# Joined transposing transfers, two kinds of square buffers and new transfer clocks in a gated-attention and token-mixer kernel

## The chip, the core and the metric

The kernel runs on one core of a Trainium2 chip. The core has a matmul engine (PE, with its weight loads shown apart as PEld), three elementwise engines (DVE, ACT and POOL), and SP, whose queue here issues most of the transfers that 16 DMA engines carry out. The metric is the time on the device of one execution, in microseconds, as the median of several runs.

## What is computed

Eight batches of 3200 rows pass through two stages. `u` and `v` have 256 columns, `z` has 64.

```python
scores = (1.0 / S) * np.matmul(z, z.transpose(0, 2, 1))
attn = np.maximum(scores, 0.0) ** 2
x = u * np.matmul(attn, v)
wq, wk = x @ w_q, x @ w_k
W_tok = (1.0 / np.sqrt(64)) * np.einsum('bsd,btd->bst', wq, wk)
mixed = np.einsum('bst,btd->bsd', W_tok, x)
out = np.maximum(mixed, 0.0) @ w_out
```

The score matrix is symmetric, since both factors are `z`. The second stage has no nonlinearity between its two products, so it is computed as wq times the small matrix that wk and x make together (the "heads"), without the matrix of 3200 x 3200.

## The kernel before

**Tiles.** A batch has 25 blocks of 128 rows. Its columns are worked in seven groups: six of 512 and a last one of 128. A score tile is one block of 128 rows against one group. Two score tiles are a pair: two matmuls on the two halves of PE's rows fill one of two PSUM buffers of two banks each (`scores`, line 263). DVE or ACT empties it through the ReLU into a float32 buffer `g` (lines 290 and 286), and ACT or POOL squares that into an fp16 buffer `at` of 1024 columns (lines 306 and 308). The second product (line 351) takes 128x128 pieces of `at` as weights and blocks of `v` as the moving operand, and sums them in four accumulator banks.

**Symmetry.** Tiles that lie across the diagonal within two groups, or towards the last group, are computed once. For the other side they are transposed by a transfer from `at` into a buffer `tt` (`ttl` for the last group; line 330). The eight-block transfer of a pair has 1024 columns. There are seven buffers `tt`, the "homes".

**Later stages.** When a half of a group's sums is complete it is copied (line 368), added (line 369) and multiplied by `u` on POOL (line 388) into `x_sb`. This is transposed by a transfer (line 400) into `xT_sb`, projected (line 417), the keys are transposed into `kx` (line 436) and doubled by POOL (line 448). Heads (line 455), mix (line 483) and output product (line 521) follow, in part beside the next batch's attention. The output is emptied by DVE or ACT (lines 546 and 551) and stored by SP (line 552). `z` of the next batch is loaded by POOL's queue with a cast, and transposed by four transfers (line 163, list `ZTURNS`) into `zT2`.

**Order.** All engines run in an order that the program writes out before it runs: a planner keeps a clock for each engine (`clock`, `give`), for SP's queue (`sp_at`) and for the transfers (`dma_at`), and adds the next instruction by these clocks. Transfers are entered by `move` with a ready time, a due time, SP's issue time and the transfer's duration, and `send` issues the one with the earliest due time. `choose` picks ACT or DVE for a score tile with the margins `BIAS` and `LATE`; `squares` picks ACT or POOL. A pair is produced when PE has a free score buffer and the `at` buffer of the pair 16 before it (`NAT`) has been used up and read out by its transfers (`all_used`, `turned_at`, `out_of`). The clocks decide only the order and the engine. On the chip the instructions wait for each other by semaphores, and each engine works its own list in that order.

```python
done + SLACK, due + SLACK, 1.28, 0.21 * n, turn,
...
sp_at[0] = max(begun + issue, dma_at[0] - RING)
if landed:
    landed(max(sp_at[0], dma_at[0]) + LANDS)
```

The last groups of the last batch and their output stages are written out by hand behind the planner's loop.

Of the kernel before, what the change touches and what calls it, by code (L numbers as in the profile page):

```python
# [16 lines left out]
def kernel(  # L17
# [15 lines left out]
    P = 128  # L33
# [17 lines left out]

    NAT = 16
    NX = 7
# [98 lines left out]
    ztimes = []  # L152
    ZTURNS = [(0, 0, 7), (1, 0, 7), (0, 7, 13), (1, 7, 13)]

# [87 lines left out]
    NPAIR = NTILE // 2  # L242
    made, turned = {}, {}
    NHOME = 7
    homes, homes_free = {}, list(range(NHOME))

# [11 lines left out]
    def scores(p, banks=None):  # L258
        assert len(ztimes) >= 4 * tiles[2 * p + 1][0] and p_chunk(p) in z_at, (p, clock, len(ztimes), z_at)
        sc = banks or ps_tile("sc")  # L260
        for h, (b, gi, ti) in enumerate(tiles[2 * p : 2 * p + 2]):
            gs, gw = starts[gi], widths[gi]
            nc.tensor.matmul(  # L263
                out=sc[h][:, 0:gw] if banks else sc[:, h, 0:gw],
                lhsT=z_cols(b, h, ti * P, P),
                rhs=z_cols(b, h, gs, gw),
                start=True,
                stop=True,
            )
        return sc  # L270
# [25 lines left out]
    def second_stage(p, g, ways):  # L296
        at = pat.tile([P, 2 * W], FP16, tag="at", name="at")
        at0 = 0
        parts = pieces(p)
        if len(ways) > len(parts):  # L300
            parts = [(slice(h, h + 1), parts[0][1]) for h in range(2)]
        for (hs, w), on_act in zip(parts, ways * 2):
# [6 lines left out]
            at0 += n * w  # L309
        at0, blocks = 0, []  # L310
        for tile_ in tiles[2 * p : 2 * p + 2]:
# [287 lines left out]
    mixed_at = []  # L599
    MIXES = 10.0  # L600
    MIXES_END = 14.0
# [7 lines left out]
    LANDS = 4.0  # L609
    RING = 2.0  # L610
    SLACK = 1.0
# [7 lines left out]
    def send(x):  # L619
# [75 lines left out]
    def squares():  # L695
        while pending and pending[0][0] <= clock[PE] + 0.3:
# [7 lines left out]
            else:  # L704
                done = give(ACT, ready, 1.06) if by_act else give(POOL, ready, 1.9)
            for (b, gi, gj, _, nn, _, _), turn in second_stage(p, g, ways):
                n = nn * widths[gi] // P
                due = done + {1: 4.0, 2: 9.0}.get(gj - gi, FARDUE)
                out_of[p] = out_of.get(p, 0) + 1
                move(  # L710
                    done + SLACK, due + SLACK, 1.28, 0.21 * n, turn,
                    lambda t, x=(p, b, gi, gj, nn): block_landed(t, *x),
                    lambda x=(b, gi, gj): has_home(*x),
                )
            for x in tiles[2 * p : 2 * p + 2]:
                row_at[x] = done + 0.6

# [14 lines left out]
    def use_keys(b, gi):  # L732
# [17 lines left out]
        if not final:  # L750
            move(
                done + SLACK, done + 10.0, 1.28, 0.21 * n, lambda: turn_keys(b, gi),
                lambda t: at_time(t, lambda: double(b, gi)),
# [63 lines left out]
    def project_out(b, gi, ps, ready):  # L817
# [13 lines left out]

        move(done + SLACK, done + 6.0, 0.55, 1.6, stores[0], landed)

    def push(takes):
        give(POOL, clock[PE], 0.6)
        dma_at[0] = max(dma_at[0], clock[PE]) + takes

    Z0 = 24
    ZWAIT, ZDUE, ZSTEP, ZSTEP0 = 14.0, 32.0, 7.0, 5.0
    V0 = 56  # L840
    V1 = 10

    def batch_begun(b, t):
        if b + 1 < B:
            t0 = max(t + 6, Z0)
            at_time(t0, lambda: (load_z(b + 1), push(3.0)))
            step = ZSTEP if b else ZSTEP0
            for i, (_, m0, m1) in enumerate(ZTURNS):
                move(
                    t0 + ZWAIT + step * i, t0 + ZDUE + step * i, 1.28, 0.21 * (m1 - m0),  # L850
                    lambda i=i: turn_z(b + 1, i),
# [6 lines left out]
    def v_loaded(b, n0, nn):  # L858
        load_v(b, n0, nn)
        push(2.5)  # L860
        for n in range(n0, n0 + nn):
            v_at[b, n] = dma_at[0] + 5.0

    z_ready = {}

    def z_here(p):
        b = tiles[2 * p + 1][0]
        return not b or z_ready.get((b, 3), 1e9) <= clock[PE]

    def group_begun(b, gi, t):  # L870
        if gi == 0:
            batch_begun(b, t)
        if gi + 1 < NG:
            move(max(t + 2, clock[POOL] + SLACK), t + 7, 0.55, 1.6, lambda: load_u(b, gi + 1))
        elif b + 1 < B:
            move(max(t + 2, clock[POOL] + SLACK), t + 7, 0.55, 1.6, lambda: load_u(b + 1, 0))

    SPARE = 0.5
    BIAS = 0.2
    XDUE = 5.0  # L880
    XWAIT = 2.0
    LATE = 0.5

    def half_done(b, gi, half):
# [10 lines left out]
        if half == halves(gi)[-1]:  # L895
            n = 8 if widths[gi] == W else 2
            move(
                t + SLACK, t + XDUE, 1.28, 0.21 * n, lambda: turn_x(b, gi),
                lambda t: x_landed(t, b, gi), lambda: len(xTs) < NXT,
# [91 lines left out]

    def all_used(p):
        return all(x in used for x in tiles[2 * p : 2 * p + 2])

# [25 lines left out]
    at_time(V3, lambda: (load_first_v(4, 8), give(POOL, clock[PE], 0.6)))  # L1020
    move(10.0, 14.0, 0.55, 1.6, lambda: load_u(0, 0))
    load_weights()
# [6 lines left out]
    while groups or work or current["left"]:  # L1029
# [18 lines left out]
        p = produced[0]  # L1048
        able = p < NPAIR and z_here(p) and z_at[p_chunk(p)] <= now and (p < NAT or all_used(p - NAT) and turned_at.get(p - NAT, 0.0) <= now and not out_of.get(p - NAT))
        wanted = able and p * total < (done_acc + lead) * NPAIR  # L1050
# [124 lines left out]
```

## Time and profile before

| | |
|---|---|
| runs | 774.49, 774.61 and 777.17 us, median 774.61 |
| profiled execution | 773.15 us, its span 770.9 us |
| granted PE clock | 0.997 |
| PE | 761.7 us busy, 12,408 matmuls |
| POOL, ACT, DVE | 591.1, 561.2 and 510.5 us busy |
| transposing transfers issued by SP | 328: 191 of `at`, 56 of `x_sb`, 53 of `qk`, 28 of `zn` |

A group's row has the source line, engine, operation, output and input, form and count; then busy time and the mean of one in ns; then the idle time of the engine just before such instructions, and what ended most of it. A row of waits has who waited, for whom, the sum in us, the number of times and the longest. A row of a timeline has start, duration, engine, line and operation; "x18" means that 18 neighbours of one kind are merged, and a bracket gives idle time before them. A tile's row has the least, median and largest duration of its instructions in ns, and a last line gives issue to landing in us. The row of a stretch has its bounds and length, then busy time and count for each engine.

### The profile page before, as it was taken

Reading aid. Unit: us, or ns where it says so; the run is one execution under the profiler, and the core shown is the slowest. Engines: PE = TensorE matmul, PEld = TensorE weight load, DVE = VectorE, ACT = ScalarE, POOL = GpSimd, SP = SyncE. Lnnn points to the kernel's source line nnn. Section 1 sums busy time; section 2 is a strip of 40 time slices with the busy share of each in tenths; the row PEclk is TensorE's granted clock in tenths of the full one; section 3 lists DMA queues with packets and bytes.
Section 4 is the critical chain, followed back from the end, with each engine's and each line's share of the span. In section 5 each row is a group of like instructions: output and inputs, shape, how many; then the busy total and the mean of one; then the engine's idle time right before and its main releaser. Section 6 shows DMA issues by size and latency. Waiting matters only on the chain.

```text
span 770.9 us, 28221 instructions
## 1 busy us (share of the span) xinstructions
PE 761.7 (99%) x12408; PEld 678.4 (88%) x12408; DVE 510.5 (66%) x537; ACT 561.2 (73%) x647; POOL 591.1 (77%) x496
## 2 busy tenths in 40 slices
PE   8999999999999999999999999999999999999996
PEld 7889998888898888989889988998889989898884
DVE  6775876675787566765677756765667476675645
ACT  7785876778758678875788677877777676777734
POOL 8796788789687778666778687887878887888740
PEclk9999999999999999999999999999999999999998
DMA  8999999999999999999899999999999998979625
GB/s 199 130 187 182 167 204 173 160 212 194 194 162 189 194 209 190 182 213 203 153 190 162 188 231 163 219 145 160 262 156 192 184 190 211 201 143 203 152 84 191
DMA packets 307114, 141.09 MB, mean 183 GB/s; under 512 B 285744, under 2 KB 288432, under 8 KB 306992
## 3 DMA queue, kind: packets, MB, share of 16 engines
q1 hardware_dynamic: 300224, 123.13, 85.0%
q0 software_dynamic: 6624, 15.98, 14.8%
q8 instruction: 97, 1.59, 0.9%
q14 instruction: 25, 0.20, 0.1%
q10 hardware_dynamic: 144, 0.20, 0.1%
HBM read 59.64 MB, written 26.21 MB: 111 GB/s over the span
## 4 chain that ended last, share of the span: by engine, by line
PE 94%; POOL 2%; DVE 1%; DMA 1%; ACT 1%; issue 1%; POOLq 0%; SPq 0%; DVEq 0%; ACTq 0%
PE acc L351 68%; PE sc L263 13%; PE fo L521 6%; PE qk L417 3%; PE qk L455 2%; POOL at L308 2%; PE mx L483 1%; DMA z<-in_z_dram 1%; POOL x_sb L388 1%; DVE g L290 0%; ACT g L286 0%; DVE fo L546 0%; DMA xT_sb<-x_sb 0%; PE hd L455 0%; ACT at L306 0%
## 5 line engine op out<-in xcount | busy, mean ns | idle before, releaser
L351 PE MATMUL acc<-v_sb,at 64*128 64x256 f16 x7344 | 504.7, 269 | 0.0
L308 POOL TENSOR_TENSOR at<-g 128x1024 f16<-128x1024 f32 (+1 forms) x218 | 402.3, 1859 | 71.6 <-ACT g L286 29.1
L351 PEld LDWEIGHTS <-at 64*128 64x128 f16 x7344 | 407.2, 94 | 48.1 <-issue 4.8
L290 DVE TENSOR_SCALAR g<-sc 128x1024 f32<-128x1024 f32 (+2 forms) x285 | 338.5, 1203 | 122.8 <-PE sc L263 114.3
L306 ACT ACTIVATE at<-g 128x1024 f16<-128x1024 f32 (+2 forms) x255 | 257.2, 1023 | 21.8 <-DVE g L290 17.8
L286 ACT ACTIVATE g<-sc 128x1024 f32<-128x1024 f32 (+2 forms) x186 | 183.2, 989 | 76.8 <-PE sc L263 75.0
L388 POOL TENSOR_TENSOR x_sb<-both,u_sb 128x512 f16<-128x512 f32 (+1 forms) x112 | 135.8, 1217 | 81.6 <-DVE both L369 77.7
L263 PE MATMUL sc<-zT 64*128 64x512 f16 x924 | 188.1, 375 | 1.4 <-DVE g L290 0.6
L351 PE MATMUL acc<-v_sb,tt 64*128 64x256 f16 x2272 | 163.4, 269 | 0.0
L351 PEld LDWEIGHTS <-tt 64*128 64x128 f16 x2272 | 126.2, 94 | 10.3
L369 DVE TENSOR_TENSOR both<-acc,both 128x512 f32<-128x512 f32 (+1 forms) x104 | 69.6, 670 | 21.4 <-ACT both L368 17.0
L263 PEld LDWEIGHTS <-zT 64*128 64x128 f16 x924 | 61.2, 94 | 7.6 <-issue 3.9
L368 ACT COPY both<-acc 128x512 f32<-128x512 f32 (+1 forms) x69 | 39.0, 565 | 38.7 <-PE acc L351 36.1
L546 DVE TENSOR_SCALAR fo<-fo 128x1024 f32<-128x1024 f32 (+1 forms) x28 | 32.4, 1166 | 46.6 <-PE fo L521 46.6
L509 ACT ACTIVATE rt<-mx 128x1024 f16<-128x1024 f32 x39 | 39.9, 1024 | 12.6 <-PE mx L483 12.1
L521 PE MATMUL fo<-wo,rt 128*128 128x256 f16 x386 | 46.6, 273 | 0.5 <-ACT rt L505 0.5
L521 PEld LDWEIGHTS <-rt 128*128 128x128 f16 x386 | 36.2, 98 | 8.4 <-issue 3.6
L431 ACT CAST qk<-qk 128x512 f16<-128x512 f32 (+1 forms) x47 | 25.3, 539 | 24.6 <-PE qk L455 20.0
L368 DVE COPY both<-acc 128x512 f32<-128x512 f32 (+1 forms) x35 | 23.6, 674 | 21.2 <-PE acc L351 19.9
L470 DVE TENSOR_TENSOR ha<-qk,ha 128x512 f32<-128x512 f32 x37 | 25.5, 689 | 14.4 <-ACT qk L431 14.1
L551 ACT ACTIVATE fo<-fo 128x1024 f32<-128x1024 f32 (+2 forms) x23 | 22.5, 978 | 16.5 <-PE fo L521 15.8
L417 PE MATMUL qk<-xT_sb,wqk 64*128 64x256 f16 (+1 forms) x404 | 32.3, 265 | 0.0
(55 smaller groups left out, 282.9 us busy)
## 6 DMA issues: line engine op xcount, KB each, us to landing
u_sb<-in_u_dram SPq DMA_DIRECT2D x48, 512.0 KB, 4.8
out_dram<-fo SPq DMA_DIRECT2D x46, 512.0 KB, 5.1
v_sb<-in_v_dram POOLq DMA_DIRECT2D x35, 320.0 KB, 6.0
zn<-in_z_dram POOLq DMA_DIRECT2D x7, 400.0 KB, 7.8
tt<-at SPq DMA_TRANSPOSE x143, 4.7
u_sb<-in_u_dram SPq DMA_DIRECT2D x8, 128.0 KB, 2.9
out_dram<-fo SPq DMA_DIRECT2D x4, 256.0 KB, 3.3
xT_sb<-x_sb SPq DMA_TRANSPOSE x56, 5.4
```

The lines of the kernel that those rows point to most:

```text
L263: nc.tensor.matmul(out=sc[h][:, 0:gw] if banks else sc[:, h, 0:gw], lhsT=z_cols(b, h, ti * P, P), rhs=z_cols(b, h, gs, gw), start=True, st ...
L286: nc.scalar.activation(out=g[:, hs, 0:w], in_=part, func=RELU, scale=GSCALE)
L290: nc.vector.tensor_scalar(out=g[:, hs, 0:w], in0=part, scalar1=0.0, scalar2=GSCALE, op0=AOP.max, op1=AOP.mult,)
L306: nc.scalar.square(out=out, in_=g[:, hs, 0:w])
L308: nc.gpsimd.tensor_mul(out=out, in0=g[:, hs, 0:w], in1=g[:, hs, 0:w])
L351: nc.tensor.matmul(out=accs[half, r][:, ds((j % 2) * D, D)], lhsT=weights(b, gi, ti, j)[top(r), :], rhs=vs[b][top(r), ti, :], start=(first ...
L368: copy(out=both[:, 0 : n * D], in_=accs[half, 0][:, 0 : n * D])
L369: nc.vector.tensor_add(out=both[:, 0 : n * D], in0=accs[half, 1][:, 0 : n * D], in1=both[:, 0 : n * D])
L388: nc.gpsimd.tensor_mul(out=xs[b, gi][:, 0:n, :, r, :].rearrange("p n c d -> p (n c) d"), in0=both[:, 0 : n * D].rearrange("p (m d) -> p m ...
L417: nc.tensor.matmul(out=ps[:, r, 0 : n * P], lhsT=wqk[top(r), c, :, :].rearrange("p t h -> p (t h)"), rhs=xTs[b, gi][top(r), 0:n, c, :], st ...
L509: nc.scalar.activation(out=out, in_=part, func=RELU)
L521: nc.tensor.matmul(out=banks[r][:, ds(j * D, D)], lhsT=flat[:, ds((dc * n + j) * P, P)], rhs=wo[:, dc, :], start=(dc == 0 and j == 0), sto ...
```

## The change

Two neighbouring pairs that both belong to one transposed block become a "two": they share one `at` buffer of 2048 columns (tag `ats`, three of them, `NAT2`), and one transfer of 16 blocks of 128 columns takes both, issued after the second square. Other pairs keep buffers of 1024 columns, of which there are now 10 instead of 16. A pair is produced when the earlier users of its own kind of buffer are done (`prior`, `has_at`). `z` is transposed in two transfers of 13 blocks instead of four of 7 and 6.

The planner's figures change: a transposing transfer of n blocks counts 1.25 us on SP and 0.2 + 0.13 n on the transfer clock (before 1.28 and 0.21 n), a plain one 0.45 and 1.7 (before 0.55 and 1.6); a transfer starts on its clock only after its issue; landing is counted from the transfer clock alone. `RING` goes from 2.0 to 1.5, `BIAS` from 0.2 to 0, `LATE` from 0.5 to 0.3, `MIXES` from 10 to 14, `V1` from 10 to 8, and pushes of POOL's queue count less.

```diff
-    NAT = 16
+    NAT = 10
+    NAT2 = 3
...
-    ZTURNS = [(0, 0, 7), (1, 0, 7), (0, 7, 13), (1, 7, 13)]
+    ZTURNS = [(0, 0, 13), (1, 0, 13)]
...
+    def block_of(p):
+        rows = [(b, gi, group_of(ti)) for b, gi, ti in tiles[2 * p : 2 * p + 2]]
+        b, gi, gj = rows[0]
+        whole = rows[0] == rows[1] and is_turned(b, gi, gj) and gj < LASTG
+        return rows[0] + (tiles[2 * p][2] - starts[gj] // P,) if whole else None
+
+    twos, prior, at_of, done_at = {}, {}, {}, {}
+    ones = []
+    for p in range(NPAIR):
+        x, y = block_of(p), block_of(p + 1) if p + 1 < NPAIR else None
+        if p - 1 in twos:
+            continue
+        if x and y and x[:3] == y[:3] and (x[3], y[3]) == (0, 2):
+            pairs = sorted(twos)
+            prior[p] = (pairs[-NAT2], pairs[-NAT2] + 1) if len(pairs) >= NAT2 else ()
+            twos[p] = p + 1
+        else:
+            prior[p] = (ones[-NAT],) if len(ones) >= NAT else ()
+            ones.append(p)
...
-        at = pat.tile([P, 2 * W], FP16, tag="at", name="at")
-        at0 = 0
+        if p in twos:
+            at = pat.tile([P, 4 * W], FP16, tag="ats", name="at", bufs=NAT2)
+            at_of[p], at_of[p + 1] = (at, 0), (at, 2 * W)
+        elif p not in at_of:
+            at_of[p] = pat.tile([P, 2 * W], FP16, tag="at", name="at"), 0
+        at, first = at_of[p]
+        at0 = first
...
+        if p in twos:
+            blocks = []
+        elif p - 1 in twos:
+            blocks = [blocks[0][:3] + (0, 4, 0, 4 * W)]
...
-    MIXES = 10.0
+    MIXES = 14.0
...
-    RING = 2.0
+    VLANDS = 5.0
+    RING = 1.5
...
-        dma_at[0] = max(dma_at[0], begun) + takes
         sp_at[0] = max(begun + issue, dma_at[0] - RING)
+        dma_at[0] = max(dma_at[0], begun + max(issue, 0.9)) + takes
         if landed:
-            landed(max(sp_at[0], dma_at[0]) + LANDS)
+            landed(dma_at[0] + LANDS)
...
+                if p - 1 in twos:
+                    done = max(done, done_at[p - 1])
                 due = done + {1: 4.0, 2: 9.0}.get(gj - gi, FARDUE)
                 out_of[p] = out_of.get(p, 0) + 1
                 move(
-                    done + SLACK, due + SLACK, 1.28, 0.21 * n, turn,
+                    done + SLACK, due + SLACK, 1.25, 0.2 + 0.13 * n, turn,
...
-    BIAS = 0.2
+    BIAS = 0.0
     XDUE = 5.0
     XWAIT = 2.0
-    LATE = 0.5
+    LATE = 0.3
...
-    def all_used(p):
-        return all(x in used for x in tiles[2 * p : 2 * p + 2])
+    def has_at(p):
+        return all(
+            all(x in used for x in tiles[2 * q : 2 * q + 2])
+            and turned_at.get(q, 0.0) <= clock[PE]
+            and not out_of.get(q)
+            for q in prior.get(p, ())
+        )
```

More of the change, by code (lines that the diff above doesn't have):

```diff
@@ L309, in second_stage @@
             at0 += n * w
-        at0, blocks = 0, []
+        at0, blocks = first, []
         for tile_ in tiles[2 * p : 2 * p + 2]:
@@ L830, in landed @@
                 stored[i] = t
-        move(done + SLACK, done + 6.0, 0.55, 1.6, stores[0], landed)
+        move(done + SLACK, done + 6.0, 0.45, 1.7, stores[0], landed)
     def push(takes):
         give(POOL, clock[PE], 0.6)
-        dma_at[0] = max(dma_at[0], clock[PE]) + takes
+        dma_at[0] = max(dma_at[0], clock[PE] + 2.0) + takes
     Z0 = 24
@@ L840 @@
     V0 = 56
-    V1 = 10
+    V1 = 8
     def batch_begun(b, t):
```

27 lines of the change are left out of this document (14 added, 13 removed).

## The prediction

> **What bounds the kernel now.** I read the page's first part first, then the busy time by stretch of the span, then who the matmul engine (PE) waited for, then the pace of its matmuls.
>
> ```profile
> span 770.9 us, 28221 instructions
> PE 761.7 (99%) x12408; PEld 678.4 (88%) x12408; DVE 510.5 (66%) x537; ACT 561.2 (73%) x647; POOL 591.1 (77%) x496
> ```
> ```profile
> core 0: us, PE busy (x) PEld busy (x) DVE busy (x) ACT busy (x) POOL busy (x), PEclk, DMA share, GB/s
> 0.00:20.00 20.00, 18.05 (x232) 14.52 (x234) 13.46 (x17) 14.29 (x18) 16.59 (x21) 1.00 0.80 194
> 20.00:60.00 40.00, 39.26 (x640) 34.63 (x638) 30.00 (x30) 31.19 (x35) 34.46 (x28) 1.00 1.07 160
> 60.00:740.00 680.00, 679.89 (x11216) 610.33 (x11213) 451.91 (x472) 505.87 (x576) 534.87 (x445) 1.00 1.04 185
> 740.00:771.00 31.00, 24.54 (x332) 18.91 (x328) 15.17 (x21) 9.84 (x21) 5.18 (x4) 0.93 0.45 162
> ```
> ```profile
> PE warm L144 <- DVE wo L996: 1.0, 1, 1.0
> PE sc L263 <- DVE g L290: 0.6, 2, 0.4
> ...
> PE qq L417 <- DMA xT_sb<-x_sb: 0.2, 1, 0.2
> ```
>
> PE shows 0.11 us of idle between 60 and 740 us, 2.7 us before that and about 6.4 us in the tail. On a transfer it waited 0.2 us in the whole run, in the tail. So the transposing transfers, which are all that the change joins, hold nothing back that the profile can see.
>
> Busy is not the same as full pace, because a matmul's 269 ns overlap the next one's. The starts tell the pace:
>
> ```profile
> 41.41 0.40 PE L263 MATMUL sc<-zT 64*128 64x512 f16 x2
> 41.62 1.16 PE L351 MATMUL acc<-v_sb,at 64*128 64x256 f16 x18
> 42.60 0.40 PE L263 MATMUL sc<-zT 64*128 64x512 f16 x2
> ```
> ```profile
> L351 PE MATMUL acc<-v_sb,at 64*128 64x256 f16 x7344 | 504.7, 269 | 0.0
> L263 PE MATMUL sc<-zT 64*128 64x512 f16 x924 | 188.1, 375 | 1.4 <-DVE g L290 0.6
> L351 PE MATMUL acc<-v_sb,tt 64*128 64x256 f16 x2272 | 163.4, 269 | 0.0
> L521 PE MATMUL fo<-wo,rt 128*128 128x256 f16 x386 | 46.6, 273 | 0.5 <-ACT rt L505 0.5
> L417 PE MATMUL qk<-xT_sb,wqk 64*128 64x256 f16 (+1 forms) x404 | 32.3, 265 | 0.0
> ```
>
> 18 accumulating matmuls from 41.62 to 42.60 are 54.4 ns each, and two scores from 41.41 to 41.62 take 0.21 us. The 7344 + 2272 accumulating matmuls at 54.4 ns are 523 us, the 924 scores 97 us, the 404 projections 22 us at the same 54.4 ns (the same 64x256 form), and the 386 of the output at about twice that (all 128 rows, so no second one runs beside it) 42 us. That is 684 us of the 761.7 busy ones; the groups that I don't show (the rest of the accumulation, heads, mix, start) are nearly all work of the same pace. What is left to win is the 2.7 us of idle before 60 us and short waits hidden inside busy time. I found one cluster of those:
>
> ```profile
> 46.63 0.40 PE L263 MATMUL sc<-zT 64*128 64x512 f16 x2
> 46.85 0.29 PE L351 MATMUL acc<-v_sb,at 64*128 64x256 f16 x2
> 46.96 0.40 PE L263 MATMUL sc<-zT 64*128 64x512 f16 x2
> 47.18 0.83 PE L351 MATMUL acc<-v_sb,at 64*128 64x256 f16 x12
> 48.42 0.87 PE L263 MATMUL sc<-zT 64*128 64x512 f16 x4 [0.41 <-DVE g L290]
> 49.11 1.49 PE L351 MATMUL acc<-v_sb,at 64*128 64x256 f16 x24
> 50.60 0.39 PE L263 MATMUL sc<-zT 64*128 64x512 f16 x2
> 50.82 0.83 PE L351 MATMUL acc<-v_sb,at 64*128 64x256 f16 x12
> 51.73 0.39 PE L263 MATMUL sc<-zT 64*128 64x512 f16 x2
> ```
>
> Twelve matmuls from 47.18 are 0.65 us, yet the next scores start 1.24 us later: 0.59 lost. Four scores should take 0.42 and take 0.69: 0.27. Then 24 take 1.49 for 1.31 and 12 take 0.91 for 0.65: 0.18 and 0.26. Sum 1.3 us. The cause: there are two score banks, and here they are asked for faster than they are emptied. The bank begun at 46.63 was free at 48.42, so a bank comes back 1.79 us after its scores begin.
>
> **The change, part by part.** I use the built program's order, row against row, for what moves; it holds no times.
>
> *Nothing leaves PE.* Both programs have the same matmuls, form by form. The tail, from the last group's scores on, stands in the same order. So the 750 or so us of pace stay.
>
> *Transfers joined.* 140 transposing transfers of 1024 columns become 70 of 2048; 50 of 512 and one of 1024 stay; z takes 14 instead of 28. That is 84 issues fewer on SP's queue:
>
> ```profile
> L330 SPq DMA_TRANSPOSE tt<-at x143: 1231/1354/5576, 17.1 to 713.4; - x143
> ...
> DMA to landing us min/median/max: 2.4/4.7/9.8
> ```
> ```profile
> L330 SPq DMA_TRANSPOSE ttl<-at x48: 1193/1262/2715, 26.4 to 723.4; - x48
> ...
> DMA to landing us min/median/max: 2.3/4.7/9.3
> ```
> ```profile
> 42.42 4.42 SPq L330 DMA_TRANSPOSE tt<-at  x3
> ```
>
> At 1.35 us each (tt; z is taken the same) SP is spared about 113 us. Its worth in the end time is 0, because PE waited 0.2 us for transfers; the cover is the distance from a transposed pair's scores to the first use of its block, which in the built orders, counted in matmuls at their pace, is 12.9 us at least before and 14.6 after, 40 us in the median of both.
>
> No 2048-column transfer stands in the trace. Below: it lands like the others, 4.7 us after issue (512 and 1024 columns both have that median). Above: like two in succession, 9.4. Three of 1024 were issued and taken within 4.42 us, so one more 1024 columns is at most 1.5 us. I take 6.2, nearer the flat end, as doubling from 512 to 1024 cost nothing in the median. The joined transfer also waits for the second square; scores of the two pairs stand 1.2 us apart in the median, 3.9 at most. Behind it on SP stand loads of u, stores, x and keys; they gain more from the missing issues than they lose by that.
>
> *Buffers.* This is where a cost could arise. 16 single buffers become 10 single and 3 double ones. A double returns only when its one transfer has been read out, and the square that takes it next waits on ACT or POOL, with evictions queued behind it on ACT; for these PE waits through the score banks. By the order, the next scores into a double stand at least 12.1 us after the last scores of its previous user (5% below 13.4, a quarter below 17.6); before, at least 16.9.
>
> ```profile
> L308 POOL TENSOR_TENSOR at<-g 128x1024 f16<-128x1024 f32 (+1 forms) x218 | 402.3, 1859 | 71.6 <-ACT g L286 29.1
> L290 DVE TENSOR_SCALAR g<-sc 128x1024 f32<-128x1024 f32 (+2 forms) x285 | 338.5, 1203 | 122.8 <-PE sc L263 114.3
> ```
> ```profile
> SPq L330 <- POOL at L308: 51.2, 37, 2.8
> ```
>
> The previous user needs 1.8 us (bank) + 1.9 (square) + 1.4 (SP's mean wait, 51.2 over 37) + 6.2 = 11.3 us; the new square starts 1.8 us after its own scores; so 9.5 us are needed and 12.1 is the least there is: covered by 2.6 us at the tightest. With the longest landing (9.8 + 1.5 = 11.3) 14.6 are needed, and about one in ten of 67 reuses, 6 or 7, would wait some 1 us each. Cost from 0 to 4 us of ACT or POOL, of which PE sees a part; I take 0.3.
>
> *Redrawn clocks.* They move the order and the choice of engine. Counted in the built order: output evictions on ACT 21 -> 42 and on DVE 25 -> 4, bank copies from ACT to DVE 22, key casts to DVE 9, POOL squares +8. At the profile's 1.02, 1.22, 0.69, 0.59 and 1.89 us the loads become about 560 for ACT, 498 for DVE, 608 for POOL: all far below PE.
>
> ```profile
> L546 DVE TENSOR_SCALAR fo<-fo 128x1024 f32<-128x1024 f32 (+1 forms) x28 | 32.4, 1166 | 46.6 <-PE fo L521 46.6
> L551 ACT ACTIVATE fo<-fo 128x1024 f32<-128x1024 f32 (+2 forms) x23 | 22.5, 978 | 16.5 <-PE fo L521 15.8
> L368 ACT COPY both<-acc 128x512 f32<-128x512 f32 (+1 forms) x69 | 39.0, 565 | 38.7 <-PE acc L351 36.1
> L368 DVE COPY both<-acc 128x512 f32<-128x512 f32 (+1 forms) x35 | 23.6, 674 | 21.2 <-PE acc L351 19.9
> ```
>
> The order decides the bank stalls. The pair of close requests of 46.6 to 48.4 is gone (banks asked back after 1.08 and 1.19 us of pace): -1.3. Two others come, near 7.4 and 16.6 us of pace, where banks are asked back after 0.97 us instead of 1.79: 0.8 each, +1.6. Between 60 and 740 us the count of banks asked back within 1.3 us is the same, 11 and 11. Bounds: all of the start's 2.7 us and the 1.3 won, or as much again lost.
>
> Sum: -1.3 + 1.6 + 0.3 = +0.6, which is nothing on 770.9. The profiled execution took 773.15 us with what lies around its span, 1.46 below the median of the three runs, 774.61. I forecast the median's 774.6 with the rounding of the sum: **774.9 us**, own range 772 to 777.5.
>
> **Rivals.** *Faster (7%).* Every wait before 60 us goes: -2.7 - 1.3 = -4.0, 770.6 us. For it: transfers land sooner on a freer queue. Against: those waits are on DVE evictions and start-up, none on a transfer. Of the 7%, 1% goes to a larger gain, down to the 678 us for which weight loads are busy, should PE's starts have free time in them; the starts at 54.4 ns of matmuls that last 269 show none. [...]
>
> *Slower: the doubles come back late (20%).* Mechanism: three doubles, each held from the first of two squares until a long transfer is read. It decides from a landing of about 9 us (12.1 available less 1.8 + 1.9 + 1.4 before the issue, plus the 1.8 that the next square starts late). With a joined transfer at 15 us (twice a crowded 7.5, between the 4.7 and 9.8 of the row) 18.3 us are needed, and over a quarter of 67 reuses, some 19, wait about 2.5 us. The squares of a double start mostly on ACT, which evicts 186 of 471 score tiles (0.39); a bank has some 0.5 us to spare (median request 2.28 against 1.79), so PE loses 19 x 2.0 x 0.39 = 15 us: 789. A milder form, a quarter to a half of it, gives 779 to 783; I take 781 as its typical time. For it: the least distance shrinks from 16.9 to 12.1 us. Against: landing hardly grew from 512 to 1024 columns.
>
> ```profile
> L286 ACT ACTIVATE g<-sc 128x1024 f32<-128x1024 f32 (+2 forms) x186 | 183.2, 989 | 76.8 <-PE sc L263 75.0
> ```
>
> *Slower by the engines' new shares (6%).* Two output tiles in succession are both emptied by ACT: the second bank comes 1.0 us later than with DVE beside it. About 21 such pairs, 0.2 to 0.4 us each of it seen by PE: +4 to +8, about 780. Against: ACT's total does not grow.
>
> *Not done.* The joined transfers stand in the built order as single instructions of 16 blocks, so the change does what it says.
>
> **How the numbers follow.** Forecast 67%, faster 7%, late doubles 20%, shares 6%. 0.5% is 3.9 us, about what a measurement can tell from no change: faster means below 770.7, slower above 778.5. Faster 0.07, within 0.67, slower 0.26. The range reaches down to 771.8, most of the start's waits, and up to 782, past the milder late doubles and the shares; the 789 case is left out.
>
> **What would show it.** Right: PE again idle under 1 us from 60 to 740; 70 tt transfers with landings of 5 to 8 us in the median; no wait of a square on a transfer; SP's tt issues near 1.4 us. Wrong: "at <- DMA tt" among ACT's or POOL's waits, scores waiting for g beyond 60 us, or tt landings above 9 us. The forecast falls if PE's idle in the middle exceeds 4 us.

## The result, and the profile after

The changed kernel is slower: 788.81 us in the median of six runs (781.06 to 790.57), against 776.30 us for six runs of the kernel before (774.49 to 777.78). The ratio is 1.0153, with a 95% interval of 1.0119 to 1.0187. The forecast was 774.9 us, in a range up to 782.0: it had the time all but unchanged, and the time rose by 12.5 us. So it was wrong. The profiled execution took 790.57 us. One slow execution of a later kernel (`XWAIT` 3.5, 794.06 us) is left out of that kernel's ratio and of its row in the table below.

The page of the kernel after, its first part and its chain (shares of the span by engine, then by line):

```profile
span 788.6 us, 28025 instructions
...
PE 767.4 (97%) x12408; PEld 666.3 (85%) x12408; DVE 500.7 (63%) x544; ACT 557.6 (71%) x630; POOL 609.5 (77%) x508
...
PE 87%; DMA 6%; POOL 2%; issue 1%; DVE 1%; ACT 1%; SPq 1%; POOLq 0%; DVEq 0%
```

PE has its 12,408 matmuls as before, and DVE, ACT and POOL carry the loads that were counted out (498, 560 and 608 us). Nothing was added to PE, yet the span is 17.7 us longer, and 6% of the chain now stand with transfers. The stretches of the span show where:

```profile
60.00:740.00 680.00, 669.63 (x10957) 584.72 (x10954) 434.24 (x467) 487.71 (x542) 537.61 (x446) 0.99 1.02 181
```
```profile
120.00:140.00 20.00, 16.89 (x258) 13.54 (x256) 10.88 (x13) 11.08 (x12) 12.68 (x12) 0.91 1.20 186
140.00:320.00 180.00, 179.95 (x2959) 157.55 (x2955) 118.64 (x128) 130.13 (x145) 148.75 (x123) 1.00 1.02 187
320.00:345.00 25.00, 22.28 (x364) 18.83 (x362) 12.84 (x14) 16.62 (x19) 17.97 (x15) 1.00 1.20 170
345.00:420.00 75.00, 75.00 (x1241) 64.95 (x1237) 47.13 (x55) 56.48 (x64) 62.99 (x50) 1.00 1.03 187
420.00:440.00 20.00, 19.36 (x312) 17.29 (x310) 11.46 (x14) 14.22 (x15) 14.60 (x14) 1.00 1.21 184
440.00:500.00 60.00, 60.00 (x996) 51.02 (x992) 36.32 (x41) 44.20 (x51) 46.52 (x40) 1.00 1.00 184
500.00:520.00 20.00, 16.36 (x229) 12.51 (x226) 11.60 (x13) 11.76 (x12) 12.13 (x11) 0.83 1.22 175
520.00:740.00 220.00, 219.78 (x3609) 191.64 (x3606) 143.00 (x153) 160.29 (x178) 174.44 (x144) 1.00 0.93 180
```

The kernel before had 11,216 matmuls done between 60 and 740 us; here there are 10,957, so 259 are late, which is 14.1 us at 54.4 ns. PE's idle time is 680 - 669.63 = 10.4 us of that. The rest is pace: from 500 to 520 us PE is 16.36 us busy, but with only 229 matmuls at a granted clock of 0.83. Nearly all of it lies in four short stretches, at 120, 320, 420 and 500 us; in the long ones between them PE is idle for 0.3 us in 535. (With every matmul charged at the usual pace of its form, those four stretches lose 15.6 us more than the same four of the kernel before.) A loss in four places is not a slower routine; something happens four times. The last two columns show that of these stretches the transfer engines are busiest in the four, 1.20 to 1.22 (the share sums the packets' times, so it can pass 1), while they move no more bytes than elsewhere. That alone does not make a loss: from 220 to 240 us the share is 1.24 and PE is never idle.

Who PE waited for, kernel after (us in all, times, longest):

```profile
PE acc L381 <- issue: 7.2, 4, 3.6
PE qk L447 <- DMA xT_sb<-x_sb: 2.9, 3, 1.4
```

These two kinds of wait are new. Three projections waited for the transposed `x`. And four times PE stood before an accumulating matmul whose operands were all there ("issue": nothing in the profile holds it). The first of these in the timeline of the kernel after:

```profile
119.54 0.42 PE L284 MATMUL sc<-zT 64*128 64x512 f16 x2
119.75 0.53 PE L381 MATMUL acc<-v_sb,at 64*128 64x256 f16 x5
122.22 0.50 PE L381 MATMUL acc<-v_sb,at 64*128 64x256 f16 x5 [1.93 <-issue]
122.45 1.05 PE L381 MATMUL acc<-v_sb,tt 64*128 64x256 f16 x8
123.09 0.84 PE L381 MATMUL acc<-v_sb,at 64*128 64x256 f16 x4
123.52 0.84 PE L284 MATMUL sc<-zT 64*128 64x512 f16 x2
123.95 2.29 PE L381 MATMUL acc<-v_sb,at 64*128 64x256 f16 x19
```

PE stops after the fifth of a run of equal matmuls, an odd number, so inside a pair; the two pairs before it start at 119.754 and 119.796, and at 119.863 and 119.905 us. What it lacked, by the numbers that follow, was instructions. The page lists a queue for instructions, with 97 packets and 1.59 MB, 16,384 bytes in each packet. The trace has 24,853 instructions of PE (weight loads, matmuls and semaphore instructions), so 1.59 MB are 64 bytes for each, and a packet of 16 KB holds 256. I numbered these instructions in the order of the trace and set the four stops beside the packets (a stop is counted from the last matmul's start to the next one's):

```
PE resumes  at instruction  mod 256  stop us | packet begins  ends    resumes after its end
122.22      3777            193      2.20    | 119.85         120.79  1.43
328.33      10433           193      1.55    | 325.82         326.85  1.48
431.26      13760           192      0.57    | 428.72         429.84  1.42
506.21      16065           193      3.91    | 503.79         504.87  1.34
```

All four stops stand at the same place modulo 256, and PE goes on 1.3 to 1.5 us after the end of a packet that came late. For three packets in four PE arrives 4.6 us or more after the packet's end. In the kernel before the least was 1.50 us, and PE idled for 0.11 us between 60 and 740 us: there it was just not held up.

Now what made them late. SP's queue and POOL's load of `z` in the kernel after, near the longest stop:

```profile
489.61 14.05 SPq L360 DMA_TRANSPOSE tt<-at  x2
```
```profile
489.84 0.59 POOL L157 DMA_DIRECT2D zn<-in_z_dram  x1
```

Two transposing transfers kept SP for 14.05 us. They began together with the load of the next batch's `z`, which converts from float32 on its way. The same place 385 us earlier:

```profile
104.15 15.16 SPq L360 DMA_TRANSPOSE tt<-at  x2
```
```profile
104.53 0.59 POOL L157 DMA_DIRECT2D zn<-in_z_dram  x1
```

In the kernel before, the load of `z` at 104.02 us met four smaller transfers, and SP was through after 7.29 us:

```profile
105.11 7.29 SPq L330 DMA_TRANSPOSE tt<-at  x4
```
```profile
104.02 0.59 POOL L156 DMA_DIRECT2D zn<-in_z_dram  x1
```

The two places shown of the kernel after belong to the longest stop and to the one at 122 us. Both times the long issue is the second of two joined transfers in succession, 11.14 and 11.27 us; the other five loads of `z` meet one joined transfer at a time, and its issue takes 5.7 us at most. The two shorter stops stand beside loads of `v`, which convert as well; for the one at 328 us:

```profile
323.58 0.59 POOL L151 DMA_DIRECT2D v_sb<-in_v_dram  x1
```
```profile
316.16 8.31 SPq L360 DMA_TRANSPOSE tt<-at  x1
```

By count of the packets, the transposes move 14 packets from 494 to 496 us in the kernel after, and 949 from 502 to 504 us, as the load of `z` ends (issued at 489.84 us, it took 13.3 us to land; the median of the seven is 6.5). Rows of the two kinds of transfer, kernel after (least, median and longest issue in ns on SP; then issue to landing in us):

```profile
L360 SPq DMA_TRANSPOSE tt<-at x73: 1249/2932/11269, 16.6 to 731.3; - x73
...
DMA to landing us min/median/max: 2.4/5.5/15.6
```
```profile
L430 SPq DMA_TRANSPOSE xT_sb<-x_sb x56: 1189/1242/5062, 32.1 to 771.1; - x56
...
DMA to landing us min/median/max: 2.3/5.9/10.8
```

The median landing of `tt` is 5.5 us, near the 6.2 that I took. The longest issue is 11.27 us, against 5.58 before, and whatever stands behind it in SP's queue waits, the transposes of `x` among them: one was issued 12.0 us after its `x` was ready. From there the second wait follows. The transposed `x` lands, in the median, 4.57 us ahead of its projection (before: 6.81), and with the least margin 0.05 us (before: 2.54). The last batch's last two groups, which are written out by hand, are not in these four figures.

### The profile page after: what moved, and what is told of

It is laid out like the page before. It is cut to its first block, busy times and chain, and to the rows that moved or that the text cites. A ratio compares the mean times of both kernels' runs of the same rounds, so it can differ in the third digit from the quotient of the medians.

```text
span 788.6 us, 28025 instructions
## 1 busy us (share of the span) xinstructions
PE 767.4 (97%) x12408; PEld 666.3 (85%) x12408; DVE 500.7 (63%) x544; ACT 557.6 (71%) x630; POOL 609.5 (77%) x508
## 3 DMA queue, kind: packets, MB, share of 16 engines
q8 instruction: 97, 1.59, 0.9%
## 4 chain that ended last, share of the span: by engine, by line
PE 87%; DMA 6%; POOL 2%; issue 1%; DVE 1%; ACT 1%; SPq 1%; POOLq 0%; DVEq 0%
PE acc L381 64%; PE sc L284 12%; PE fo L551 6%; PE qk L447 3%; DMA xT_sb<-x_sb 3%; PE qk L485 2%; DMA tt<-at 2%; PE mx L513 1%; DMA v_sb<-in_v_dram 1%; POOL x_sb L418 1%; DVE g L311 1%; POOL at L334 1%; DMA z<-in_z_dram 1%; ACT g L307 0%; ACT at L332 0%
## 5 line engine op out<-in xcount | busy, mean ns | idle before, releaser
L334 POOL TENSOR_TENSOR at<-g 128x1024 f16<-128x1024 f32 (+2 forms) x230 | 420.7, 1843 | 66.9 <-DVE g L311 56.1
L381 PEld LDWEIGHTS <-at 64*128 64x128 f16 x7344 | 398.0, 94 | 64.1 <-issue 13.2
L311 DVE TENSOR_SCALAR g<-sc 128x1024 f32<-128x1024 f32 (+1 forms) x280 | 331.9, 1198 | 175.8 <-PE sc L284 166.4
L332 ACT ACTIVATE at<-g 128x1024 f16<-128x1024 f32 (+2 forms) x245 | 246.0, 1023 | 24.1 <-DVE g L311 20.9
L398 DVE COPY both<-acc 128x512 f32<-128x512 f32 (+1 forms) x59 | 39.6, 672 | 51.9 <-PE acc L381 50.2
L581 ACT ACTIVATE fo<-fo 128x1024 f32<-128x1024 f32 (+2 forms) x44 | 41.7, 996 | 14.1 <-PE fo L551 14.1
L398 ACT COPY both<-acc 128x512 f32<-128x512 f32 (+1 forms) x45 | 25.5, 566 | 31.8 <-PE acc L381 31.4
L478 POOL COPY kx<-kx 128x128 f16<-128x128 f16 (+1 forms) x99 | 25.5, 287 | 26.3 <-DMA kx<-qk 26.2
L461 ACT CAST qk<-qk 128x512 f16<-128x512 f32 (+1 forms) x36 | 19.4, 540 | 31.9 <-PE qk L485 28.5
L485 PE MATMUL qk<-x_sb,kx 64*128 64x256 f16 x360 | 29.0, 269 | 0.0
```

Source lines behind the costliest of these rows:

```text
L311: nc.vector.tensor_scalar(out=g[:, hs, 0:w], in0=part, scalar1=0.0, scalar2=GSCALE, op0=AOP.max, op1=AOP.mult,)
L332: nc.scalar.square(out=out, in_=g[:, hs, 0:w])
L334: nc.gpsimd.tensor_mul(out=out, in0=g[:, hs, 0:w], in1=g[:, hs, 0:w])
L381: nc.tensor.matmul(out=accs[half, r][:, ds((j % 2) * D, D)], lhsT=weights(b, gi, ti, j)[top(r), :], rhs=vs[b][top(r), ti, :], start=(first ...
L398: copy(out=both[:, 0 : n * D], in_=accs[half, 0][:, 0 : n * D])
L485: nc.tensor.matmul(out=ps[:, r, D : 2 * D], lhsT=ks[b, gi][top(r), n, :, :].rearrange("p a h -> p (a h)"), rhs=x_rows(b, gi, n)[top(r), :, :],
```

## The experiments

The theory that came out of the profile: the order that the redrawn clocks make leaves too little time from a finished `x` to its projection; when a converting load makes the transposing transfers crawl, the transposed `x` and PE's own instructions come late. The rivals: the long joined transfers do it by themselves; the three doubles are too few; or the new order is one bad draw, and any other would be as good as the old one.

To compare orders without times, I counted in each built program PE's matmuls between the last accumulation of half a group and the first projection of its `x`, at the pace of their forms. Below this is "the distance": 19.1 us in the median before (lower quarter 16.9), 15.8 after (14.7). In the trace of the kernel after, the median `x` takes some 3.4 us to be finished, 1.7 to be issued and 5.9 to land: 11.0 us. Its slowest twentieth is issued 9.3 us late or later, which makes 18.6.

**The joined transfer taken apart.** Same order, buffers and clocks; each joined transfer is issued as two of 1024 columns, one right after the other.

```diff
+            if nn == 4:
+                for h in range(2):
+                    nc.sync.dma_start_transpose(
+                        out=out[:, 8 * h : 8 * (h + 1), :], in_=at[:, 2 * W * h : 2 * W * (h + 1)]
+                    )
+                return
```

> Changed kernel with each joined transfer of 2048 columns issued as two of 1024, one directly behind the other; buffers, order and clocks are those of the change. Theory A (the long transfer crawls beside a cast load of v and keeps back the fetch of PE's instructions; PE runs dry at multiples of 256 instructions): the waits of 2 to 4 us at such places are gone or under 1 us in all, time 774 to 779 us. Rival B (the doubles come back late): same buffers, so the time stays 786 to 790. Rival C (the new order and clocks cost it, whatever the transfers' length): stays 786 to 790.

Measured: 788.92 us (782.75 to 791.13, 4 runs), ratio 1.017 (1.0121 to 1.022). The expected return to 774 to 779 did not come. Its profiled run, at 782.75 us the fastest of the four:

```profile
PE qk L453 <- DMA xT_sb<-x_sb: 6.5, 5, 2.3
```
```profile
L362 SPq DMA_TRANSPOSE tt<-at x140: 1231/1310/4892, 25.4 to 724.2; - x140
```

No issue is longer than 4.89 us, and PE's waits in this run, listed down to 0.3 us, have none for "issue". That does not make the stops a matter of the joined length: with `XWAIT` 5, further down, the same separate transfers have two of 1.5 and 0.7 us. And the waits for `xT_sb` more than doubled, from 2.9 to 6.5 us, with 143 issues of `tt` on SP for 73. The loss is the same, in the other of its two forms. So the joined transfer alone is not the cause.

**z taken apart**, alone and with the joined transfers: one transfer of 13 blocks becomes one of 7 and one of 6.

```diff
-        nc.sync.dma_start_transpose(
+        for m0, m1 in ((0, 7), (7, 13)):
+            nc.sync.dma_start_transpose(
```

> Changed kernel with each z transfer of 13 blocks issued as two of 7 and 6; the transfers of 2048 columns stay. Theory A: the four long waits of the profile lie beside loads of v and transfers of at, not of z, so at most a few us are won: 784 to 790 us. If the z transfers are the cause: 774 to 779. Rivals B and C: 786 to 790.

> Changed kernel with both kinds of long transfer issued in pieces of at most 1024 columns. Theory A: no fetch of instructions is late by more than 1 us, 774 to 778 us, at or below the time with only the at transfers in pieces. Rivals B and C: 786 to 790.

Measured: 792.99 us (789.75 to 795.4, 4 runs), ratio 1.0233 (1.0198 to 1.0268), and with both taken apart 793.23 us (789.74 to 796.15, 4 runs), ratio 1.0224 (1.0189 to 1.0258). PE waited 11.8 and 15.3 us for `xT_sb`. Both times lie above all that I had expected (790 at most). They are some 4 us above the change and above the joined transfers taken apart (788.81 and 788.92): fewer issues for `z` are worth something, in this order.

**No loads of v** after the first batch: all batches use batch 0's `v`, which leaves out seven of the eight batches' `v`.

```diff
-        load_v(b, n0, nn)
+        vs[b] = vs[0]
```

> Changed kernel that leaves out the loads of v for batches 1 to 7 and uses the v of batch 0 in all batches; the transfers stay joined. Theory A: without cast loads beside them the joined transfers do not crawl (longest SP issue of one under 7 us instead of 11 to 14), no fetch is late, 773 to 777 us. If length alone delays the fetch: still 784 to 790. Rival B: a little better with shorter landings, 780 to 788. Rival C: 786 to 790.

Measured: 781.89 us (780.13 to 783.56, 4 runs), ratio 1.0092 (1.0064 to 1.0119). Kernel without loads of `v`, waits of PE and SP's timeline:

```profile
PE acc L381 <- issue: 4.0, 1, 4.0
...
PE qk L447 <- DMA xT_sb<-x_sb: 0.8, 1, 0.8
```
```profile
481.51 14.17 SPq L360 DMA_TRANSPOSE tt<-at  x2
```

Some two fifths of the loss go, and with them three of the four stops, among them the two beside loads of `v`. I had blamed `v` alone and expected 773 to 777 us with no long issue; the one stop of 4.0 us that stays follows a pair of transfers that took 14.17 us beside the load of `z`, with an issue of 11.28 us among them.

**No loads of z** after batch 1: batches 2 to 7 use batch 1's `z`, so their scores are those of another batch.

```diff
-            at_time(t0, lambda: (load_z(b + 1), push(2.4)))
+            at_time(t0, lambda: (load_z(b + 1) if b == 0 else None, push(2.4)))
```

> Changed kernel that leaves out the loads of z for batches 2 to 7 and uses the z of batch 1 there; nothing else differs. Theory A (cast loads of z or v beside a joined transfer make it crawl and keep back PE's instructions): the 11 us issue near 490 us is gone, the longest there is under 7 us and PE does not run dry there (3.6 us dry and some 2 us of half clock before); the one of batch 1, near 108 us, stays. Time 778 to 785 us. If a joined transfer keeps back the instructions by itself: PE is dry there as before, 785 to 791.

Measured: 776.1 us (773.3 to 784.73, 10 runs), ratio 1.0007 (0.9969 to 1.0045): the loss is gone, with the order, the joined transfers, the doubles and the short distance as they were. In its profiled run no projection waited for `xT_sb`. One stop of PE was left, 1.5 us, after a `tt` issue of 10.21 us beside a load of `v`. I had expected the long issue near 108 us to stay; it went too, as the load of `z` at 104.53 us is already that of batch 2.

**Only the planner's figures, with the old transfers and buffers**, and the reverse. The first kernel is the one before with the new figures (its `LATE` kept at 0.5); the second is the one after with all old figures.

```diff
-    MIXES = 10.0
+    MIXES = 14.0
...
-    RING = 2.0
+    VLANDS = 5.0
+    RING = 1.5
...
-            landed(max(sp_at[0], dma_at[0]) + LANDS)
+            landed(dma_at[0] + LANDS)
...
-    BIAS = 0.2
+    BIAS = 0.0
```

> Kernel before with its 16 single buffers, transfers of at most 1024 columns and z in four, but with the redrawn clocks (LATE stays at 0.5). Theory D: PE waits for xT for 5 to 15 us as with the transfers in pieces, 784 to 794 us. If the joined transfers or the doubles are the cause: 773 to 778.

> Joined transfers, z in two, 3 double and 10 single buffers as in the change, but every figure of the planner as before the change. Theory D (the redrawn clocks make the order count on earlier landings: projections wait for xT, and PE's instructions are fetched late in the packed stretches): PE waits for xT and runs dry for under 1.5 us in all, 773 to 778 us. Theory B (doubles) or the joined transfers themselves: 784 to 792.

Measured: new figures on the old kernel 795.81 us (792.09 to 799.98, 4 runs), ratio 1.0221 (1.0151 to 1.0291); old figures on the new kernel 795.55 us (794.51 to 797.06, 4 runs), ratio 1.0235 (1.018 to 1.029). Waits of PE, first in the former, then in the latter:

```profile
PE qk L417 <- DMA xT_sb<-x_sb: 11.4, 5, 3.1
PE acc L351 <- POOL at L308: 6.0, 4, 2.1
```
```profile
PE sc L284 <- DVE g L311: 9.2, 15, 1.2
PE fo L551 <- DVE g L311: 1.8, 3, 1.2
```

The figures alone bring the loss, and its wait for `xT_sb`, to transfers that are not joined. The joined transfers under the old figures lose as much, but at another place: the score banks come back late fifteen times, and nothing waits for `xT_sb`. I had expected 773 to 778 us there, had the figures been the only cause, and 784 to 792 had the doubles or the joined transfers been it; the result lies above both. Squares on ACT and POOL waited for no transfer in its profiled run, so no double came back late to them. It is the kind of loss that the prediction looked for in the order: counted in its built program, the order asks a bank back within 1.3 us some 30 times between 60 and 740 us, where the prediction counted 11 before and 11 after. Why the old figures make such an order of the joined transfers stays open.

**More time for x.** Two ways, each a single figure of the changed kernel: the planner's landing of every transfer (`LANDS`), or its wait between a landed `x` and the projection (`XWAIT`, line 915).

```diff
-    LANDS = 4.0
+    LANDS = 6.0
```

> Changed kernel with one figure altered: the planner counts 6 us instead of 4 from the transfer clock to a landing. Theory D: the projections stand later behind xT, PE's wait for xT falls from 2.9 us to under 0.5; late fetches may remain, 776 to 786 us. If xT's lateness only follows from something else: 786 to 791.

```diff
-    XWAIT = 2.0
+    XWAIT = 5.0
```

> Changed kernel with one figure altered: a projection is planned 5 us instead of 2 behind the planned landing of its xT. Theory D: no wait for xT; the fetches stay late as before (about 7 us of dry PE and some 4 of half clock), so 780 to 786 us. If waits for xT do not matter: 786 to 791.

Measured: 774.54 us (772.84 to 779.12, 10 runs), ratio 0.9975 (0.9947 to 1.0004), and 774.51 us (772.82 to 777.98, 10 runs), ratio 0.9972 (0.9943 to 1.0001). Both give the whole loss back, with joined transfers and three doubles. The first waits of PE with `LANDS` 6, and its `tt` issues:

```profile
PE warm L145 <- DVE wo L1035: 1.0, 1, 1.0
PE sc L284 <- ACT g L307: 0.7, 2, 0.3
PE sc L284 <- DVE g L311: 0.6, 1, 0.6
```
```profile
L360 SPq DMA_TRANSPOSE tt<-at x73: 1249/3089/6769, 16.7 to 711.4; - x73
```

The span is 770.9 us, that of the kernel before. I had expected late instruction packets to remain (776 to 786 us with `LANDS` 6, 780 to 786 with `XWAIT` 5), and missed: in both orders a load of `z` meets one joined transfer at a time, the longest issue is 6.8 and 6.9 us, and no stop is left.

**The same margin on the other transfers, and taken from the kernel before.** `XWAIT` 5 with the joined transfer issued as two; `XWAIT` 5 on the kernel before with the new figures; and `XWAIT` 2 to -2 on the kernel before, nothing else.

```diff
-    XWAIT = 2.0
+    XWAIT = -2.0
```

> Changed kernel with the joined transfer of a square buffer issued as two of 1024 columns and a projection planned 5 us instead of 2 behind the landing of xT. If the lateness of xT was what the pieces still cost (788.9 us): 773 to 778. If the order has other losses that only the joined transfers avoid: 780 to 788.

> Kernel before with the redrawn clocks (795.8 us) and a projection planned 5 us behind xT's landing. Theory D: PE's wait for xT falls from 11.4 us to under 1; the waits for squares on POOL (6.0 us) may stay: 776 to 786 us. If the redrawn clocks cost by the engines' shares instead: 790 to 798.

> Kernel before with one figure altered: a projection is planned 2 us before instead of 2 behind the planned landing of xT. Theory D: the least measured time from xT's landing to its use, 2.5 us before, falls to nothing; PE waits for xT 3 to 12 us in all, 779 to 790 us. If xT's margin is not what matters: 774 to 778.

Measured: 779.88 us (775.6 to 785.39, 10 runs), ratio 1.0053 (1.0011 to 1.0095); 787.1 us (785.49 to 788.51, 4 runs), ratio 1.0123 (1.0072 to 1.0175); and 780.45 us (775.69 to 787.32, 10 runs), ratio 1.0058 (1.0022 to 1.0095). The first stays above what I had expected of a cure (773 to 778), and the second, at 1.0123 for 1.0221 without the margin, keeps more than half of its loss, although its wait for `xT_sb` falls from 11.4 to 1.8 us. So on transfers of 1024 columns more margin does not give the whole loss back. PE's waits for "issue" in the first, where no transfer is joined:

```profile
PE acc L387 <- issue: 1.5, 1, 1.5
...
PE sc L284 <- issue: 0.7, 1, 0.7
```

As in the kernel after, nothing in the profile holds PE there, and the longest issue of a `tt` is 8.51 us. In the last the kernel before, with its distance cut to 15.7 us, shows the wait that it hardly had, and one for "issue":

```profile
PE qk L417 <- DMA xT_sb<-x_sb: 4.3, 2, 2.3
...
PE acc L351 <- issue: 0.9, 1, 0.9
```

**Margin or a bad draw.** Each such figure moves the whole order. So two controls move the order and leave the distance (`LATE` alone, and `LATE` with `BIAS`), one kernel shortens the distance, and one lengthens it by half as much as `XWAIT` 5.

```diff
-    LATE = 0.3
+    LATE = 0.5
```

> Control: the changed kernel with only LATE 0.3 -> 0.5. It moves the order (about a quarter of the rows of PE and SP stand elsewhere) and leaves the distance from a half group's last accumulating matmul to its projection: median 15.9 us of PE's pace against 15.8, lower quarter 14.9 against 14.7. Theory margin: it stays slow, 783 to 793 us, with waits of PE for xT_sb or dry stretches. Rival luck (the changed kernel's order was one bad draw, and any other order does as well as those with the larger margin): 773 to 778.

```diff
-    BIAS = 0.0
+    BIAS = 0.2
...
-    LATE = 0.3
+    LATE = 0.5
```

> Second control: LATE 0.3 -> 0.5 and BIAS 0 -> 0.2, the figures of the kernel before for the choice of engine; the distance stays at 15.8 us in the median, 14.9 in the lower quarter. Theory margin: 783 to 793. Rival luck: 773 to 778.

```diff
-    XWAIT = 2.0
+    XWAIT = 0.0
```

> The changed kernel with XWAIT 2 -> 0: the distance falls to 13.6 us in the median, 12.8 in the lower quarter. Theory margin: slower than the changed kernel, 800 to 815 us, PE waiting for xT_sb over 15 us in all. Rival luck: anywhere, 775 to 795, with waits for xT_sb no larger than before.

```diff
-    XWAIT = 2.0
+    XWAIT = 3.5
```

> Half the dose: XWAIT 2 -> 3.5; distance 17.2 us in the median, 16.5 in the lower quarter, against 17.5 and 16.5 of the kernel with LANDS 6. Theory margin: 774 to 779, PE waiting for xT_sb under 1 us. Rival luck: no better placed than the two controls.

Waits of PE in the two controls and in the shortened one, in this order:

```profile
PE acc L381 <- issue: 4.1, 2, 3.7
PE qk L447 <- DMA xT_sb<-x_sb: 2.9, 3, 1.8
```
```profile
PE qk L447 <- DMA xT_sb<-x_sb: 6.1, 4, 3.4
```
```profile
PE qk L447 <- DMA xT_sb<-x_sb: 16.6, 7, 3.7
```

The kernels with joined transfers and the new figures, by distance:

| kernel | distance, median (lower quarter) us | time us (range, runs) | ratio (95%) |
|---|---|---|---|
| `XWAIT` 0 | 13.6 (12.8) | 799.65 (796.92 to 800.73, 4) | 1.0314 (1.0279 to 1.0348) |
| the change | 15.8 (14.7) | 788.81 (781.06 to 790.57, 6) | 1.0153 (1.0119 to 1.0187) |
| `LATE`, `BIAS` old | 15.8 (14.9) | 785.11 (780.56 to 790.78, 4) | 1.0135 (1.0074 to 1.0196) |
| `LATE` old | 15.9 (14.9) | 783.61 (777.08 to 786.13, 10) | 1.0088 (1.006 to 1.0117) |
| `XWAIT` 3.5 | 17.2 (16.5) | 779.34 (776.65 to 783.3, 7) | 1.0061 (1.0031 to 1.0092) |
| `LANDS` 6 | 17.5 (16.5) | 774.54 (772.84 to 779.12, 10) | 0.9975 (0.9947 to 1.0004) |
| `XWAIT` 5 | 18.5 (17.7) | 774.51 (772.82 to 777.98, 10) | 0.9972 (0.9943 to 1.0001) |

Both controls stay slow with the known waits, and the time falls with the distance, over 25 us. A bad draw of the changed kernel's order alone does not explain that, though two controls are few. The size is not settled by the distance alone: the controls are up to 5 us better than the change at the same distance, and the two on either side (799.65 and 779.34) miss what I had expected by under 1 us. No kernel is surely faster than the one before: the two best have intervals that just reach 1.

## Why the prediction was wrong

*Nothing leaves PE; the engines' loads; the landing.* Right. The matmuls are the same, the loads came out within 3 us of 498, 560 and 608, the median landing is 5.5 us for 6.2 taken. PE waited 1.7 us for `g` in all, against 0.9 before, near the small cost that the sum had.

*Buffers.* Right in its small cost. In the kernel after, one square waited for a transfer to read its buffer, on POOL, for 3.2 us; ACT never did.

```profile
POOL at L334 <- DMA tt<-at: 3.2, 1, 3.2
```

The bound on the landing was wrong (15.6 us against 11.3), but no other late landing held up a square. So two of the signs that I had named against the forecast came, such a wait and landings above 9 us; the second could tell nothing, as the kernel before has landings up to 9.8. "The doubles come back late" gives 789 us in its full form, close to the measured time, and yet it isn't what happened: `LANDS` 6 and `XWAIT` 5 have the same three doubles and lose nothing.

*Transfers joined: "Its worth in the end time is 0 ... the cover is the distance from a transposed pair's scores to the first use of its block".* The first step that failed. That is the cover of `tt`, and it held. SP's queue also carries the transposes of `x`, which had a least margin of 2.54 us, and I gave them one sentence: "they gain more from the missing issues than they lose by that". Its premise was 113 us spared on SP, 84 issues at 1.35. Measured, an issue of `tt` takes 2.93 us in the median, where I had expected some 1.4, and SP's issues of `tt` and `z` sum to 284.5 us, against 319.4 before: 35 us spared. And an average does not tell what the longest issue does to the one transfer behind it: 1.5 us was my upper bound for another 1024 columns, and the longest joined issue, beside a load of `z`, took 11.27, against 5.58 for the longest before. A wait of 0.2 us says nothing of the margin behind it, which was 2.5 us.

*Redrawn clocks.* The step that failed by most. I asked the new order for two things, engine loads and how soon score banks are asked back, and found both unchanged. I did not ask it how far a projection stands behind its `x`, though the same count of matmuls gives it: 19.1 us before, 15.8 after. What shortened it is not that a landing is counted from the transfer clock alone: by the changed `send` that clock always stands behind SP's, so the later of the two would be the same. A likely cause is the cheaper transfer (0.2 + 0.13 x 8 = 1.24 us for an `x`, 1.68 before), which makes the planner's queue shorter; no run takes the figures apart. With the trace's 11.0 us for a median `x`, and 18.6 for its slowest twentieth, a wait could have been foreseen. The runs price it: `XWAIT` -2 alone on the kernel before brings a ratio of 1.0058, and with joined transfers and the new figures the loss is gone at 17.5 us or more. The figures on the old transfers bring 1.0221, of which more margin gives back less than half, so there the distance is not all of it.

*What no step contained:* that PE's own instructions come by transfers as well (the page's instruction queue, 97 packets, 0.9% of the 16 engines' time), and that four of those packets came late where the transposes did. In the profiled run the stops are 7.2 us and the half pace behind two of them some 4.5 (half of 3.4 and of 5.6 us); the waits for `xT_sb` are 2.9. The share of each differs from run to run and kernel to kernel (taken apart, the transfers lose as much by `xT_sb` alone), and the runs don't divide it further.

*The joining.* The length of the transfer by itself is not what costs: in one and the same order, joined against taken apart, joining is worth nothing in the new order (788.81 and 788.92 us) and 5.4 us with `XWAIT` 5 (774.51 and 779.88, ratios 0.9972 and 1.0053). But joined transfers and doubles under the old figures lose as much as a ratio of 1.0235, so the joining does cost through the order that a planner makes of it. The sign by which the forecast was to fall, PE idle over 4 us in the middle, is what the trace shows, 10.4.

Shown is, for the changed kernel: its loss needs the loads of `z` (without them 1.0007), and it goes with more distance (0.9975 and 0.9972). How much of the second is the margin itself, and how much that in the new orders no load of `z` meets two joined transfers in succession, the runs do not divide. Only argued is by what way a converting load makes transposes and instruction packets crawl; loads without a conversion weren't tried. Open are also why the order asks for the score banks so soon when the old figures meet the joined transfers, and what the new figures still cost on the old transfers when the margin is given back.

## What to carry to other kernels

When an order moves, ask it for the distance of every consumer from its producer that goes through a shared queue, not only for that of the transfers that the edit names: a wait of 0.2 us in the profile says nothing of the 2.5 us of margin behind it. Price a longer transfer by its worst neighbour on the queue (here a converting load, met by two joined transfers in succession: 11.3 us against a median of 2.9), and see what stands behind it. And a planner's constants are part of the kernel: one of them, two or three microseconds off, cost more here (1.0153 against 0.9972 with `XWAIT` 5) than 84 saved transfers brought in any run.

## What the hardware showed that was not expected

PE ran out of instructions, at the same place modulo 256 each time, for 0.6 to 3.9 us, while transposes and a converting load kept the transfer engines at a share of 1.20 to 1.22; in the kernel before PE came to a packet as little as 1.5 us after its end. Stops with nothing in the profile to hold PE occur without a joined transfer too: 0.9 us in the kernel before with `XWAIT` -2, and 1.5 and 0.7 us with the joined transfers taken apart and `XWAIT` 5. Where the packets stood there is not shown.

After the stops of 2.2 and 3.9 us PE worked at half pace for some 3.4 and 5.6 us (in the timeline above, four matmuls from 123.09 to 123.52 us are 107 ns each): the granted clock was 0.50 from 122.66 to 126.06 us, and again from 504.95 us, while PE still stood, to 511.77 us. After the stops of 0.6 and 1.5 us PE kept its pace, and the granted clock stayed at 1.00. The length of the gap does not decide it alone: with `XWAIT` 0 PE once stood idle for 3.66 us, and the granted clock stayed at 1.00 then and after:

```profile
547.00:552.00 5.00, 1.34 (x26) 1.05 (x23) 2.57 (x4) 1.35 (x2) 4.83 (x4) 1.00 1.17 292
552.00:556.00 4.00, 4.00 (x66) 3.20 (x63) 1.38 (x2) 3.53 (x5) 0.57 (x3) 1.00 1.27 223
```

Where the clock was halved, a stop of 2.2 us cost nearly twice its length: 3.4 us at half pace are 1.7 us lost.
